# Later loads of x^T and u, and one-hot blocks of 32 columns in bursts of four sets, in a gated mix of a Fourier layer and a product-key expert layer

## The chip, the cores and the metric

The kernel runs on one core of one Trainium2 chip. The metric is the device time of one execution in microseconds (us). A core has TensorE (PE in the profile; its weight loads are shown apart as PEld), VectorE (DVE), ScalarE (ACT), GpSimd (POOL) and SyncE (SP), which here only issues transfers. All work from instruction streams of their own, in order, and wait for one another by semaphores.

## The reference

For x of 2048 tokens by 640 the output is g A + (1 - g) B, a gate for each token between two layers:

```python
g = _sigmoid((x * gate_w).sum(-1, keepdims=True))
# A: Fourier mixing
a = jnp.einsum("bsd,ed->bse", x, dft_hid_re)
b = jnp.einsum("bsd,ed->bse", x, dft_hid_im)
y = jnp.einsum("ts,bse->bte", dft_seq_re, a) - jnp.einsum("ts,bse->bte", dft_seq_im, b)
# B: 32 heads, two key tables of 16, 256 experts
q = jnp.einsum("nd,dhc->nhc", xf, w_q)
s1 = jnp.einsum("nhd,ed->nhe", q1, k1)
s2 = jnp.einsum("nhd,ed->nhe", q2, k2)
...  # the two best of 16 in each table, the two best of the 4 sums, their expert numbers top_e
g = _softmax(top_s, axis=-1)
act = _gelu(jnp.einsum("nd,nhkd->nhk", xf, u[top_e]))
out = jnp.einsum("nhk,nhk,nhkd->nd", g, act, v[top_e])
```

## The kernel before

All large products are made of fp32 values split into two fp32r parts, high and low, with three matmuls each (`mm3`, L141): 128 weight columns by 512 moving columns. TensorE's stream is written out by hand and is nearly one unbroken row of them.

**The main loop.** `pieces` are 128 steps (two DFT matrices, four column blocks of 512 tokens, 16 row blocks). `seq_piece(n)` issues the load of piece n + 5, the split of piece n + 3 (ScalarE copies the high part, GpSimd, or a GpSimd transfer that adds, makes the low one) and 15 matmuls. After each piece, `follow(n)` runs whatever `at(n, f)` has entered for that piece, in the order of entry. The instruction order of every engine and queue follows from this.

**Work between the pieces, first stage (pieces 0 to 29).** The weights W of the scores (w_q times the keys) are made in eight groups of four loads: `load_wq` brings 640 KB each on SP's queue into one of five buffers, `w_part` makes 8 small matmuls (L380; 32 weight columns by 320 moving columns) from each, `split_w` and `make_t` split the result. Group G stands at piece 6 + 3G, the last at 27. Beside them stand the row blocks of x being stored for later (`put_x`), the load of x^T's first pair of token blocks (`load_xT(0)`, at piece 21), its split (`split_xT`, 27) and sums (`sum_xT`, 28), and the five blocks of u's table (`load_u(k)` at pieces 21 to 25 into two small buffers, `split_u(k)` two pieces later).

**Second stage (to about piece 66).** `score_step` makes the scores of two token blocks in four steps, `topk` picks on VectorE, `gates` and `weigh` turn the picks into three rows for each choice: a bit for the first index, a bit for the second, a weight. `rows(b)` transposes them by transfers into `ROWS[0]` and `ROWS[1]` (tokens 0 to 1023 and 1024 to 2047), the last of them spaced out by `bg.space`.

**Third stage: `experts()`.** The sums of weights for each token and expert are made by matmuls of one-hot blocks. A chunk is 64 tokens of a half (`todo`: 2 halves of 16 chunks). `build` makes a set for one chunk with three VectorE operations over 1024 fp16 elements (L845): compare the first bits with a table of 16 powers, compare the second bits, multiply the first by the weights. The innermost dimension holds 4 tokens beside one another. `use` runs a group of sets as one burst of matmuls (L857), 16 for each set, 64 weight columns by 64 moving columns (16 indices by 4 tokens on both sides), with outputs at partitions 0 or 64. Only the blocks in which a token meets itself count: `mask` (L815) multiplies by a mask on ScalarE, four operations for each chunk, and `add_up` (L821) reduces over the 4 tokens on VectorE into `cd`. There are four sets (`free_sets`, `HOT`); a group has three of them, and the next set is built before the group's burst is issued. `store_gates` stores `cd` to DRAM with two transfers for each half. Near the end (`ending`, piece 121 on) sets 2 and 3 are given up and groups have two sets.

**The pump.** Third-stage work is not placed by piece. `run_bg(0.68)` after every three matmuls adds 0.95 x 0.68 us to a credit; a generator such as `experts()` issues its next step whenever the credit is above 0, and each `yield` says what the step costs (0.8 us, later 1.05, for an operation of `build`; 0.75 for an `add_up`). `experts()` starts with a debt of 3.0. Other VectorE work lowers the credit too (`bg.credit -= ...`). So the place of a burst in TensorE's stream is fixed when the program is made, by these prices, and not by when VectorE is done.

**Fourth stage.** After piece 127 two times 42 steps with the hidden DFT and v's table make the output.

Of the kernel before, what the change touches and what calls it, by code (L numbers as in the profile page):

```python
# [33 lines left out]
NB = 4  # L34
GSCALE = 32768.0
# [4 lines left out]
NSTEP = 7 * KZ  # L40
AHEAD = 5
AWAY = 11
BYPASS = 4
ACCUM_END = NT * (NC + 2) - 4

# [61 lines left out]
def gated_mix_kernel(ctx: ExitStack, tc: tile.TileContext, xT, xn, dreT, dimT, wsre, wsim, wq, kT, uT, vv, gw, out):  # L107
    nc = tc.nc
    ctx.enter_context(tc.manual_schedule())

    const = ctx.enter_context(tc.tile_pool(name="const", bufs=1))
    big = ctx.enter_context(tc.tile_pool(name="big", bufs=1))
# [37 lines left out]
    gd = [dram.tile([2, 4, E, E, P], F32, name=f"gd{g}", tag=f"gd{g}") for g in range(2)]  # L150
# [4 lines left out]
    def run_bg(us):  # L155
# [6 lines left out]
    UH, UL = (WU[:, 2 * NW + n * KD * NE:2 * NW + (n + 1) * KD * NE].rearrange("p (k c) -> p k c", k=KD)  # L162
              for n in range(2))
# [32 lines left out]
    def at(n, f, *args):  # L196
        then.setdefault(n, []).append(lambda: f(*args))
# [4 lines left out]


    banks = []
    p3, last_part, ending, closing, early, share = None, False, False, False, True, 0.95
    grow, staged, P22 = {}, {}, {}

    def load_row(q):
# [40 lines left out]
    for q in range(2 * NC):  # L249
        n = NT * (q + 1)  # L250
# [10 lines left out]
    p1 = p1_stack.enter_context(tc.tile_pool(name="p1", bufs=1, reuse_waits="tile"))  # L261
# [77 lines left out]
    wtab4 = const.tile([P, E, 4], F16)  # L339
    powers = const.tile([P, E], F16)  # L340
    top_bits = const.tile([P, 1], F32)
    mask4 = const.tile([P, 4], F32)

    def put_keys():
        for r in range(2):
# [6 lines left out]
    def make_tables():  # L352
        for e in range(E):
            nc.gpsimd.memset(powers[:, e:e + 1], 2.0 ** (E - 1 - e))
        nc.gpsimd.memset(top_bits, INF)
        nc.gpsimd.tensor_copy(wtab4, powers[:, :, None].to_broadcast([P, E, 4]))
        nc.vector.tensor_reduce(mask4, identf.rearrange("p (a b) -> p b a", b=4), op=OP.add, axis=AX.X)
        nc.vector.tensor_scalar(mask4, mask4, 1.0 / GSCALE, None, op0=OP.mult)

    for n, f in ((2, put_keys), (4, make_ident), (9, make_tables)):  # L360
        at(n, f)
# [3 lines left out]
    WQB = 5  # L365
# [48 lines left out]
        for n in range(1, 5):  # L414
            split(t[:, n - 1], *(w[:, :, c] for w in TW[n]), nc.vector)

    uf = {}

    def load_u(k):
        uf[k] = p1.tile([P, NE], F32, name="uf", tag="uf", bufs=2)  # L420
        nc.sync.dma_start(uf[k], uT[k])

    def split_u(k):
        split(uf.pop(k), UH[:, k], UL[:, k], nc.vector)


    xf, xs = {}, {}
# [58 lines left out]
    for G in range(NG):  # L486
        b = 6 + 3 * G
# [19 lines left out]
    def gate():  # L507
# [18 lines left out]
    ROWS = [cp.tile([P, 3, P, 8], F16, name=f"rows{g}") for g in range(2)]  # L526
# [251 lines left out]
    for n in range(2 * NT + 3, 4 * NT + 3):  # L778
        s = n % NT
# [12 lines left out]

    def store_gates(g):
        if g in summed and g not in stored:
            for s in range(2):
                nc.sync.dma_start(gd[g][s].rearrange("t e f m -> e t f m"), summed[g][64 * s:64 * s + 64])
            stored.add(g)

    free_sets = deque(range(4))
# [2 lines left out]
    def experts():  # L802


        shp = [P, 16, E, 4]
        wt = wtab4[:, None].to_broadcast(shp)
        todo = deque((g, c) for g in range(2) for c in range(16))
        cd = {}

        masked, unmasked = deque(), deque()  # L810

        def mask(t):
            f = t.rearrange("p m (e t) -> p (m e) t", t=4)
            for n in range(4):
                nc.scalar.activation(f[:, :, n], f[:, :, n], AF.Copy, scale=mask4[:, n:n + 1])  # L815

        def add_up(g, c, t):
            if c == 0:
                store_gates(g - 1)
                cd[g] = p3.tile([P, E, P], F32, name="cd", tag="cd")  # L820
            nc.vector.tensor_reduce(cd[g][:, :, 8 * c:8 * c + 8].rearrange("p e m -> p m e"),  # L821
                                    t.rearrange("p m (e t) -> p m e t", e=E), op=OP.add, axis=AX.X)
            if c == 15:
                summed[g] = cd[g]

        def settle(force=False):
            us = 0.0
            if masked:
                add_up(*masked.popleft())
                us = 0.75  # L830
            if unmasked and (force or not closing):
                masked.append(unmasked.popleft())
                mask(masked[-1][2])
            return us

        def build(g, c, s):
            pt, qt = (HOT[s // 2][:, s % 2, n].rearrange("p (m e t) -> p m e t", e=E, t=4) for n in range(2))

            def row(n):
                r = ROWS[g][:, n, 8 * c:8 * c + 8, :].rearrange("p b (s t) -> p (b s) t", t=4)  # L840
                return r[:, :, None, :].to_broadcast(shp)

            assert rowed >= set(range(8 * g, 8 * g + 8))
            for o, a, b, op in ((pt, row(0), wt, OP.is_equal), (qt, row(1), wt, OP.is_equal), (pt, pt, row(2), OP.mult)):
                nc.vector.tensor_tensor(o, a, b, op=op)  # L845
                yield (0.8 if early else 1.05) + settle()

        def use(group):
            assert not last_part
            while masked or unmasked:  # L850
                yield settle(True)
            for i, (g, c, s) in enumerate(group):
                t = bank((6, 7, 5)[i], (P, 8, E * 4))
                pt, qt = (HOT[s // 2][:, s % 2, n].rearrange("p (m c) -> p m c", m=16) for n in range(2))
                for m in range(16):
                    r = slice(64 * (m % 2), 64 * (m % 2) + 64)
                    nc.tensor.matmul(t[r, m // 2, :], pt[:, m], qt[:, m], start=True, stop=True)  # L857
# [372 lines left out]
    prep_split = {NPC - 4: (0,), NPC - 3: (1,), NPC - 2: (2,), NPC - 1: (3, 4)}  # L1230
    WP = None
    for n in range(N0, NPC):
        ending, closing, early = n >= NPC - 7, n % NT == NT - 1, n < ACCUM_END
        seq_piece(n)
        follow(n)
        if n >= N1 and p3 is None and NT // NB - 1 in gated:
            p2_stack.close()
            p3 = ctx.enter_context(tc.tile_pool(name="p3", bufs=1, reuse_waits="tile"))
            pools.append(p3)
            HOT.append(p3.tile([P, 2, 2, 16 * E * 4], F16, name="hot0"))  # L1240
            HOT.append(p3.tile([P, 2, 2, 16 * E * 4], F16, name="hot1", tag="WP"))
            bg.add(experts(), late=True)
            bg.credit -= 3.0
        if n == NPC - 4:
            bg.drain(lambda: {2, 3} <= set(free_sets))
            HOT.pop()
# [57 lines left out]
```

## Time and profile before

| | us |
|---|---|
| median of 3 runs (749.87 to 751.22) | 750.1 |
| the profiled execution | 750.43 |
| its span on the core | 748.7 |
| W products, TensorE (L380, 256 matmuls) | 19.1 busy |
| one-hot matmuls (L857, 512) | 10.2 busy |
| one-hot builds, VectorE (L845, 64 and 32 operations) | 57.8 and 31.6 busy |
| masks, ScalarE (L815, 128) | 43.1 busy |
| reductions, VectorE (L821, 32) | 21.7 busy |

The span is what the profiler sees on the core; the execution's time has a little around it. A matmul's shown length is longer than its distance to the next one, since matmuls are pipelined; distances between starts are what the stream costs. In the row of a group, `x512 | 10.2, 197 | 0.0` means 512 instructions, 10.2 us busy in total, 197 ns mean of one, and no idle time of the engine ahead of them. "SPq" is SyncE's queue of transfers.

### The profile page before, as it was taken

The numbers are of one execution on the slowest core, as the hardware profiler recorded it, in microseconds if no ns is written. First come the engines' busy times: TensorE is split into PE (matmuls) and PEld (weight loads), VectorE is DVE, ScalarE is ACT, GpSimd is POOL, SyncE is SP. The second block draws the span as 40 slices with busy tenths as digits, with TensorE's granted clock in tenths as the row PEclk, the third lists the DMA queues.
The fourth block names the chain that finished last, engine by engine and source line by source line (L and its number), as shares of the span: only waits on it lengthen the run. The fifth ranks groups of instructions, "written<-read, shape, count | busy, mean of one in ns | idle before, by whom it ended". The sixth has DMA issues, their size and how long they took to land.

```text
span 748.7 us, 11141 instructions
## 1 busy us (share of the span) xinstructions
PE 743.8 (99%) x3925; PEld 603.8 (81%) x3925; DVE 585.7 (78%) x741; ACT 365.9 (49%) x664; POOL 342.4 (46%) x286
## 2 busy tenths in 40 slices
PE   9999999999999999999999999999999999999998
PEld 7777767888888888888888888888888888888887
DVE  6964098495999899999999888979899974357651
ACT  4325234543544745555463686633545653443451
POOL 5533325440532424145235456643455793487253
PEclk9999999999999999999999999999999999999999
DMA  9999999777556786972398766488876689775301
GB/s 333 392 380 364 344 374 354 231 222 250 129 176 141 190 242 157 237 200 79 114 395 285 162 168 188 133 255 280 266 234 197 222 262 343 219 239 172 113 29 71
DMA packets 84488, 171.11 MB, mean 229 GB/s; under 512 B 16080, under 2 KB 21328, under 8 KB 84176
## 3 DMA queue, kind: packets, MB, share of 16 engines
q1 hardware_dynamic: 70960, 146.13, 57.9%
q0 software_dynamic: 5472, 9.96, 8.5%
q10 hardware_dynamic: 8000, 14.31, 5.2%
q8 instruction: 31, 0.51, 0.3%
q14 instruction: 25, 0.20, 0.1%
HBM read 136.40 MB, written 32.39 MB: 225 GB/s over the span
## 4 chain that ended last, share of the span: by engine, by line
PE 94%; DMA 5%; SPq 0%; DVE 0%; ACT 0%; issue 0%; ACTq 0%
PE b L143 30%; PE b L145 30%; PE b L144 30%; PE b L239 2%; DMA wf<-in_wsre 2%; PE b L380 2%; DMA wq<-in_wq 1%; PE b L857 1%; DMA xd<-X 1%; DMA gdr<-gc 1%; DVE wp L386 0%; SPq L177 0%; ACT WS L295 0%; ACTq L514 0%; DVE ST L1191 0%
## 5 line engine op out<-in xcount | busy, mean ns | idle before, releaser
L143 PE MATMUL b<-WS,X 128*128 128x512 f32 x620 | 243.3, 392 | 0.0
L144 PE MATMUL b<-WS,X 128*128 128x512 f32 x620 | 241.4, 389 | 0.0
L145 PE MATMUL b<-WS,X 128*128 128x512 f32 x620 | 241.3, 389 | 0.0
L139 POOL TENSOR_TENSOR WS<-wf,WS 128x512 fp32r<-128x512 f32 x89 | 131.9, 1486 | 168.3 <-ACT WS L138 151.8
L143 PEld LDWEIGHTS b<-WS,X 128*128 128x128 f32 x620 | 116.3, 188 | 28.2 <-issue 4.1
L145 PEld LDWEIGHTS b<-WS,X 128*128 128x128 f32 x620 | 116.4, 188 | 24.4
L144 PEld LDWEIGHTS b<-WS,X 128*128 128x128 f32 x620 | 116.4, 188 | 23.6
L138 ACT ACTIVATE WS<-wf 128x512 fp32r<-128x512 f32 x89 | 55.5, 626 | 69.0 <-PE b L145 40.9
L845 DVE TENSOR_TENSOR hot<-rows,wtab 128x1024 f16<-128x1024 f16 x64 | 57.8, 930 | 4.3 <-PE b L857 4.3
L139 POOL TENSOR_TENSOR xl<-xf,xh 128x640 fp32r<-128x640 f32 x16 | 27.2, 1702 | 72.0 <-ACT xh L138 72.0
L567 ACT ACTIVATE sc<-b 128x512 f32<-128x512 f32 x32 | 19.9, 621 | 80.8 <-PE b L145 77.0
L191 POOL DMA_DIRECT2D WS<-in_wsre x30 | 26.4, 881 | 61.8 <-ACT WS L189 60.5
L139 POOL TENSOR_TENSOR WS<-ra,WS 128x512 fp32r<-128x512 f32 x33 | 47.1, 1439 | 14.3 <-ACT WS L138 14.1
L815 ACT ACTIVATE b<-b,mask 128x128 f32<-128x128 f32 x128 | 43.1, 342 | 14.9 <-PE b L857 11.8
L138 ACT ACTIVATE WS<-ra 128x512 fp32r<-128x512 f32 x47 | 29.4, 631 | 42.4 <-PE b L145 29.6
L622 DVE TENSOR_TENSOR eq<-sc,mm 128x1024 f16<-128x1024 f32 x32 | 44.4, 1387 | 0.9
L629 DVE TENSOR_REDUCE tied<-eq 128x64 f32<-128x1024 f16 x32 | 39.0, 1219 | 0.9
L620 DVE TENSOR_REDUCE mm<-sc 128x64 f32<-128x1024 f32 x32 | 38.7, 1211 | 0.2
L139 POOL TENSOR_TENSOR WP<-ra,WP 128x512 fp32r<-128x512 f32 x13 | 19.2, 1490 | 31.0 <-ACT WP L138 30.9
L217 DVE SCALAR_TENSOR_TENSOR ST<-ST,grow 128x512 f32<-128x512 f32 x40 | 31.7, 855 | 1.7 <-ACT tw L138 1.7
L845 DVE TENSOR_TENSOR hot<-hot,rows 128x1024 f16<-128x1024 f16 x32 | 31.6, 986 | 0.0
L143 PE MATMUL b<-WU,xh 128*128 128x512 f32 x80 | 31.1, 389 | 0.0
(209 smaller groups left out, 1449.1 us busy)
## 6 DMA issues: line engine op xcount, KB each, us to landing
X<-xd SPq DMA_DIRECT2D x36, 640.0 KB, 6.5
wq<-in_wq SPq DMA_DIRECT2D x32, 640.0 KB, 7.1
wf<-in_wsim SPq DMA_DIRECT2D x64, 256.0 KB, 4.8
wf<-in_wsre SPq DMA_DIRECT2D x63, 256.0 KB, 6.4
ra<-pd SPq DMA_DIRECT2D x40, 256.0 KB, 3.3
pd<-ST ACTq DMA_DIRECT2D x35, 256.0 KB, 5.6
WS<-in_wsre POOLq DMA_DIRECT2D x30, 256.0 KB, 6.0
xd<-X SPq DMA_DIRECT2D x11, 640.0 KB, 9.1
```

The lines of the kernel that those rows point to most:

```text
L138: nc.scalar.activation(h, f, AF.Copy)
L139: eng.tensor_sub(l, f, h.bitcast(F32))
L143: nc.tensor.matmul(o, wh, ah, start=first, stop=False, skip_group_check=more)
L144: nc.tensor.matmul(o, wh, al, start=False, stop=False, skip_group_check=more)
L145: nc.tensor.matmul(o, wl, ah, start=False, stop=last, skip_group_check=more)
L191: nc.gpsimd.dma_start(l, (wsre, wsim)[w][c, s], accum_op=OP.add)
L217: nc.vector.scalar_tensor_tensor(f, f, -1.0 if w else 1.0, g, op0=OP.mult, op1=OP.mult)
L620: nc.vector.tensor_reduce(m, sc, op=OP.max, axis=AX.X)
L622: nc.vector.tensor_tensor(eq, sc, m[:, :, None].to_broadcast([P, HH, E]), op=OP.is_equal)
L629: nc.vector.tensor_reduce(tied[:, s, ib, :], eq, op=OP.add, axis=AX.X)
L815: nc.scalar.activation(f[:, :, n], f[:, :, n], AF.Copy, scale=mask4[:, n:n + 1])
L845: nc.vector.tensor_tensor(o, a, b, op=op)
```

## The change

There are two independent edits.

The first moves x^T's first pair and u's table. The pair's load goes from piece 21 to 25, where it stands behind the last of W's loads in SP's queue, its split from 27 to 28, its sums from 28 to 29. u's five loads of 128 KB become one of 640 KB at piece 25 into one of W's five buffers, and its five splits become one at piece 27.

The second changes the one-hot blocks. With `TB = 2` the innermost dimension holds 2 tokens instead of 4, so that a set's matmuls are 32 of 32 weight columns by 32 moving columns, at output partitions 0, 32, 64 and 96 (`CG = 4`). Two sets fill one bank. A group has four sets, with two in the ending, and the banks rotate. The mask has two operations for two chunks, the reduction one for two chunks, the store four transfers for each half. A fifth set may be added (`free_now`): for the first half of the tokens in the space of `xl`, if all rows are placed and the piece is before 86 (`late`), for the second half over `ROWS[0]`, as soon as no set of the first half is left to build. The price of an operation of `build` goes from 0.8 to 0.9 in the early part, and `settle` is called once for each set instead of three times.

```diff
+TB = 2
+MS = 64 // TB
+CG = P // (TB * E)
...
-    uf = {}
-
-    def load_u(k):
-        uf[k] = p1.tile([P, NE], F32, name="uf", tag="uf", bufs=2)
-        nc.sync.dma_start(uf[k], uT[k])
-
-    def split_u(k):
-        split(uf.pop(k), UH[:, k], UL[:, k], nc.vector)
+    uf = []
+
+    def load_u():
+        f = p1.tile([P, 4, HALF], F32, name="wq", bufs=WQB).rearrange("p a b -> p (a b)").rearrange("p (k c) -> p k c", k=KD)
+        nc.sync.dma_start(f, uT.rearrange("k p c -> p k c"))
+        uf.append(f)
+
+    def split_u():
+        split(uf.pop(), UH, UL, nc.vector)
...
-    at(n - 8, load_xT, 0)
-    for k in range(KD):
-        at(n - 8 + k, load_u, k)
-        at(n - 6 + k, split_u, k)
+    at(n - 4, load_xT, 0)
+    at(n - 4, load_u)
+    at(n - 2, split_u)
     for a in range(2):
-        at(n - 2, split_xT, 0, a)
-    at(n - 1, sum_xT, 0)
+        at(n - 1, split_xT, 0, a)
+    at(n, sum_xT, 0)
...
-            for n in range(4):
-                nc.scalar.activation(f[:, :, n], f[:, :, n], AF.Copy, scale=mask4[:, n:n + 1])
+            for n in range(TB):
+                nc.scalar.activation(f[:, :, n], f[:, :, n], AF.Copy, scale=mask_t[:, n:n + 1])
...
+        def free_now():
+
+            if todo[0][0] == 1:
+                if not HOT[4:] or HOT[4][0] == 0:
+                    if HOT[4:] and 4 not in free_sets:
+                        return [s for s in free_sets if s < 2 or not ending]
+                    if not HOT[4:]:
+                        HOT.append(None)
+                        free_sets.append(4)
+                    HOT[4] = 1, ROWS[0].rearrange("p a b c -> p (a b c)")[:, :16 * P].rearrange("p (n c) -> p n c", n=2)
+            elif not HOT[4:] and not late and len(rowed) == NT:
+                HOT.append((0, big.tile([P, 2, 16 * P // 2], F16, name="hot4", tag="xl")))
+                free_sets.append(4)
+            return [s for s in free_sets if s not in ((2, 3) if ending else (4,) if late and todo[0][0] == 0 else ())]
...
-                yield (0.8 if early else 1.05) + settle()
+                yield (0.9 if early else 1.05) + (settle() if op == OP.mult else 0.0)
...
-                t = bank((6, 7, 5)[i], (P, 8, E * 4))
-                pt, qt = (HOT[s // 2][:, s % 2, n].rearrange("p (m c) -> p m c", m=16) for n in range(2))
-                for m in range(16):
-                    r = slice(64 * (m % 2), 64 * (m % 2) + 64)
-                    nc.tensor.matmul(t[r, m // 2, :], pt[:, m], qt[:, m], start=True, stop=True)
-                unmasked.append((g, c, t))
+                if i % 2 == 0:
+                    t = bank(5 + rotate("hot", 3), (P, 16, E * TB))
+                    unmasked.append((g, c, t))
+                pt, qt = (f.rearrange("p (m c) -> p m c", m=MS) for f in pair(s))
+                for m in range(MS):
+                    r = slice(TB * E * (m % CG), TB * E * (m % CG + 1))
+                    nc.tensor.matmul(t[r, 8 * (i % 2) + m // CG, :], pt[:, m], qt[:, m], start=True, stop=True)
...
-            while todo and len(group) < (2 if ending else 3):
-                free = [s for s in free_sets if s < 2 or not ending]
-                if prev and (not free or ending and any(s > 1 for g, c, s in prev)):
+            while todo and (len(group) < (2 if ending else 4) or len(group) % 2):
+                free = free_now()
+                if prev and (not free or ending and any(s in (2, 3) for g, c, s in prev)):
...
+        ending, closing, early, late = n >= NPC - 7, n % NT == NT - 1, n < ACCUM_END, n >= NT * (NC + 2) - 10
```

More of the change, by code (lines that the diff above doesn't have):

```diff
@@ L204, in gated_mix_kernel @@
     banks = []
-    p3, last_part, ending, closing, early, share = None, False, False, False, True, 0.95
+    p3, last_part, ending, closing, early, late, share = None, False, False, False, True, False, 0.95
     grow, staged, P22 = {}, {}, {}
@@ L355, in make_tables @@
         nc.gpsimd.memset(top_bits, INF)
[L356 to L358 removed]
+        nc.gpsimd.tensor_copy(wtab, powers[:, :, None].to_broadcast([P, E, TB]))
+        nc.vector.tensor_reduce(mask_t, identf.rearrange("p (a b) -> p b a", b=TB), op=OP.add, axis=AX.X)
+        nc.vector.tensor_scalar(mask_t, mask_t, 1.0 / GSCALE, None, op0=OP.mult)
     for n, f in ((2, put_keys), (4, make_ident), (9, make_tables)):
@@ L794, in store_gates @@
         if g in summed and g not in stored:
-            for s in range(2):
-                nc.sync.dma_start(gd[g][s].rearrange("t e f m -> e t f m"), summed[g][64 * s:64 * s + 64])
+            for s in range(CG):
+                n, t = divmod(TB * s, 4)
+                nc.sync.dma_start(gd[g][n, t:t + TB].rearrange("t e f m -> e t f m"),
+                                  summed[g][TB * E * s:TB * E * (s + 1)])
             stored.add(g)
@@ L802, in experts @@
     def experts():
-        shp = [P, 16, E, 4]
-        wt = wtab4[:, None].to_broadcast(shp)
+        shp = [P, MS, E, TB]
+        wt = wtab[:, None].to_broadcast(shp)
         todo = deque((g, c) for g in range(2) for c in range(16))
@@ L1232, in gated_mix_kernel @@
     for n in range(N0, NPC):
-        ending, closing, early = n >= NPC - 7, n % NT == NT - 1, n < ACCUM_END
+        ending, closing, early, late = n >= NPC - 7, n % NT == NT - 1, n < ACCUM_END, n >= NT * (NC + 2) - 10
+        assert n < NT * (NC + 2) - 1 or not HOT[4:] or HOT[4][0] or 4 in free_sets
         seq_piece(n)
@@ L1239, in gated_mix_kernel @@
             pools.append(p3)
-            HOT.append(p3.tile([P, 2, 2, 16 * E * 4], F16, name="hot0"))
-            HOT.append(p3.tile([P, 2, 2, 16 * E * 4], F16, name="hot1", tag="WP"))
+            for t in ("hot0", "WP"):
+                f = p3.tile([P, 2, 2, 16 * E * 4], F16, name="hot", tag=t)
+                HOT.extend(f[:, a] for a in range(2))
             bg.add(experts(), late=True)
```

19 lines of the change are left out of this document (11 added, 8 removed).

## The prediction

> **What bounds the kernel now.** I read the page's first part, the chain that ended last, the windows of 12 us, and then the starts of TensorE's instructions where they become irregular.
>
> ```profile
> span 748.7 us, 11141 instructions
> PE 743.8 (99%) x3925; PEld 603.8 (81%) x3925; DVE 585.7 (78%) x741; ACT 365.9 (49%) x664; POOL 342.4 (46%) x286
> PE 94%; DMA 5%; SPq 0%; DVE 0%; ACT 0%; issue 0%; ACTq 0%
> 84.00:96.00 12.00, 12.00 (x76) 8.71 (x75) 1.34 (x3) 2.45 (x5) 3.86 (x3) 1.00 1.02 414
> 96.00:108.00 12.00, 11.31 (x72) 7.90 (x70) 11.86 (x21) 3.67 (x9) 4.21 (x3) 1.00 0.98 374
> ```
>
> A window row gives its bounds and length, the busy time of PE, PEld, DVE, ACT and POOL, the granted clock, the DMA share and GB/s. TensorE is busy for 743.8 of 748.7 us, and of these two windows the second lacks 0.69 us of it. So an edit pays only where it takes time out of TensorE's own stream or a wait out of TensorE; work saved on the others is worth nothing by itself. Two places of that stream are touched:
>
> ```profile
> 97.25 10.08 DMA wq<-in_wq
> 104.86 1.82 PE L380 MATMUL b<-wq,kp 128*32 128x320 f32 x24
> 107.37 0.74 PE L380 MATMUL b<-wq,kp 128*32 128x320 f32 x8 [0.69 <-DMA wq<-in_wq]
> 108.05 0.50 PE L143 MATMUL b<-WS,X 128*128 128x512 f32 x1
> 118.55 2.29 PE b L380 x32
> ...
> 419.32 0.39 PE L145 MATMUL b<-WS,X 128*128 128x512 f32 x1
> 419.64 0.95 PE L857 MATMUL b<-hot 128*64 128x64 f16 x48
> 420.52 0.50 PE L143 MATMUL b<-WS,X 128*128 128x512 f32 x1
> 420.85 0.39 PE L144 MATMUL b<-WS,X 128*128 128x512 f32 x1
> ...
> 586.79 0.39 PE L145 MATMUL b<-WS,X 128*128 128x512 f32 x1
> 587.10 0.69 PE L857 MATMUL b<-hot 128*64 128x64 f16 x32
> 587.73 0.50 PE L143 MATMUL b<-WS,X 128*128 128x512 f32 x1
> 588.07 0.39 PE L144 MATMUL b<-WS,X 128*128 128x512 f32 x1
> 588.30 0.40 PE L145 MATMUL b<-WS,X 128*128 128x512 f32 x1
> ```
>
> A row's first number is a start, its second a length; lengths overlap, so I use starts. First place: group 6 of the W products has 32 matmuls, the last 8 of which wait for W's load 27. It takes 108.05 - 104.86 = 3.19 us, the next group 2.29: **0.90 us are lost**. Second place: the one-hot bursts. Ordinary matmuls start 0.23 us apart (588.07 to 588.30). The burst of 48 takes 420.85 - 419.32 - 2 x 0.23 = 1.07 us out of the stream, the burst of 32 takes 588.07 - 586.79 - 0.46 = 0.82. Sixteen matmuls therefore cost 0.25 us, 16 ns each, and each burst has a fixed 1.07 - 0.77 = 0.30 us. There are 512 matmuls in ten bursts of 48 and one of 32: 8.2 + 3.3 = **11.5 us**.
>
> **Part 1, loads behind W's last weights.**
>
> ```profile
> 92.96 0.87 SPq L371 DMA_DIRECT2D wq<-in_wq  x2
> 93.92 0.85 SPq L433 DMA_DIRECT2D xf<-in_xT  x2
> 94.82 0.42 SPq L421 DMA_DIRECT2D uf<-in_uT  x1
> 97.25 2.00 SPq L371 DMA_DIRECT2D wq<-in_wq  x2
> 106.63 0.33 SPq L421 DMA_DIRECT2D uf<-in_uT  x1
> 107.59 0.86 SPq L371 DMA_DIRECT2D wq<-in_wq  x2
> 113.53 0.42 SPq L371 DMA_DIRECT2D wq<-in_wq  x1
> SPq L421 <- DVE tt L408: 4.0, 2, 3.3
> ```
>
> Counted back from load 31 at 113.53, the two issues from 97.25 are loads 27 and 28, and 27 lands at 107.33 by the chain. Two xT issues (128 x 640 fp32, 0.33 MB each) and u's first (0.13 MB) stand ahead of it: 0.79 MB, 2.1 us at the 374 GB/s of that window. Without them it lands near 105.2. Its matmuls would begin at 104.86 + 0.75 x 2.29 = 106.6, so the whole 0.90 us goes and 1.4 us of slack stays. What is late next is load 31, for the last group. It too comes forward, because SP no longer stands in line at u's buffer (4.0 us in the last row): its own buffer was last read by group 6's third quarter. I take **-0.9**; if another transfer keeps load 27 late it is 0, and more than 0.9 isn't there to gain.
>
> Moved past: the two xT issues, five u issues that become one of 0.66 MB, five ACT copies and five VectorE subtractions that become one each, and xT's split and sums one piece later. u's new buffer was last read by load 27's matmuls, so SP waits for nothing beyond about 107; behind it stand pieces' loads, which have two pieces (6.8 us) in hand. ScalarE's split of u waits for a transfer that now starts with the last W loads, and behind it stand xT's split and W_seq pieces' copies, three pieces ahead of their matmuls. The price is nothing while those leads last; if u or xT lands 3 us too late it is up to 1.5 us, for the scores that start four pieces later.
>
> **Part 2, blocks of 32 columns.**
>
> ```profile
> L380 PE MATMUL b<-wq,kp 128*32 128x320 f32 x256 | 19.1, 436 | 0.7 <-DMA wq<-in_wq 0.7
> ```
>
> There are twice as many matmuls (1024) with 32 weight columns and 32 moving columns each, now four beside one another instead of two: 256 rounds before and after. A round costs 2 x 16 = 32 ns now. At the stream's rate (0.23 us for 512 columns, 0.45 ns each) 64 columns are 29 ns of it, and 3 ns are fixed. No row shows a round of 32 fp16 columns. Bounds: half a round, 16 ns (4.1 us saved); or 16 ns for each matmul as now, 64 ns a round (8.2 us lost). The nearest row for four beside one another is the W product above: 32 matmuls of 320 fp32 columns in 2.29 us, eight rounds of four, 72 ns for each, although one lasts 436. The number of instructions isn't the price there; columns are. I take columns plus the fixed part, 14.5 + 3 = 17.5, say 18 ns: 256 x 14 = **-3.6**.
>
> The Trainium skill, "TensorE: Matmul & The Clock Gate", section "Wait — 56ns, not 53.3ns?", says that starts never come closer than about 25 ns however few the columns. The 48 matmuls here, 16 ns apart on average, show that this can't hold across matmuls in different columns of the array; whether it holds for a round no run here shows. Read as a floor for a round, it would save 256 x 7 = 1.8 us instead of 3.6 (an estimate from that page).
>
> **Part 3, bursts of four sets.** 32 chunks in fours make 8 bursts, not 11: 3 x 0.30 = **-0.9** (9 bursts, if the last ones break up near the end: -0.6). The evacuation shrinks: 32 masking operations instead of 128 on ScalarE, 16 reductions instead of 32 on VectorE, both off the path, and that helps a little in Part 4.
>
> **Part 4, what a burst waits for.** Before, three sets are used after a fourth has been built, so VectorE may lag one set. The fifth set would keep that up, but it can't for the first half: it is allowed before piece 86 and only when all rows are placed.
>
> ```profile
> 422.71 2.53 ACT L246 ACTIVATE ST<-b 128x512 f32<-128x512 f32 x5
> 453.14 1.93 ACT L721 ACTIVATE rows<-lb 128x384 f16<-128x384 f16 x1
> 417.62 1.78 DVE L845 TENSOR_TENSOR hot<-hot,rows 128x1024 f16<-128x1024 f16 x1
> 420.52 0.68 DVE L845 TENSOR_TENSOR hot<-hot,rows 128x1024 f16<-128x1024 f16 x1
> 445.72 0.88 PE b L857 x48
> 446.58 0.68 DVE L845 TENSOR_TENSOR hot<-hot,rows 128x1024 f16<-128x1024 f16 x1
> L845 DVE TENSOR_TENSOR hot<-rows,wtab 128x1024 f16<-128x1024 f16 x64 | 57.8, 930 | 4.3 <-PE b L857 4.3
> L845 DVE TENSOR_TENSOR hot<-hot,rows 128x1024 f16<-128x1024 f16 x32 | 31.6, 986 | 0.0
> L845 DVE TENSOR_TENSOR hot<-rows,wtab x64: 674/681/2248, 410.1 to 572.3; 128x1024 f16<-128x1024 f16 x64
> L627 DVE TENSOR_TENSOR eq<-eq,powers x32: 678/692/3415, 155.5 to 396.7; 128x1024 f16<-128x1024 f16 x32
> L622 DVE TENSOR_TENSOR eq<-sc,mm x32: 1210/1225/2544, 151.7 to 395.5; 128x1024 f16<-128x1024 f32 x32
> ```
>
> The five copies at 422.71 close piece 79, which ends near 424. A piece is 15 x 0.23 = 3.4 us, so piece 86 starts near 424 + 6 x 3.4 + 2 bursts = 446.6; the last row is placed at 453.14. So chunks 0 to 15 run on four sets, all four go into each burst, and bursts 1 to 3 have nothing built ahead; from the fourth on, set five (over the first half's rows) restores the lag.
>
> Burst 1: the twelfth operation (420.52 + 0.68) ends at 421.2. The pump pays 0.9 instead of 0.8 for each of 12 operations, and spends 0.65 in each 0.68 us of products: with the 3.0 that it starts in debt, 13.8 of credit instead of 12.6 put the burst two steps later, at 419.32 + 0.23 + 1.36 = 420.9. With the signal's way it waits some 0.5 us. Bursts 2 and 3: before, the operation that the after kernel would wait for ended 1.5 us behind burst 3 (446.58 + 0.68 against 445.72), and 12 x 0.1 = 1.2 us of added price covers most of it; I take 0.5 each. That is **+1.5**; from 0 to a whole set for each burst (three operations of 0.93 us, the mean of the 96: 57.8 + 31.6 us): 8.4.
>
> The price of an operation itself: runs of two equal-stepped fp16 elements instead of four. Runs of four (L845, 681 ns) and of sixteen (L627, 692 ns) cost the same, so I take the same for two; the other bound is L622's 1225 ns.
>
> **Sum**, against the profiled execution (750.43 us, of which 748.7 are span): -0.9 - 3.6 - 0.9 + 1.5 = -3.9, so 746.5. The median of the runs is 750.1, 0.3 below, and the forecast goes with it: **746.3**. Its own range, from the smaller terms: 744.5 to 748.0.
>
> **Rivals.**
> 1. A round has a floor. Whatever fills a round beside its columns may not shrink with them; the 3 ns fixed speak against, and that no round under 64 columns is in the trace speaks for. Midway between 18 and 32 ns, 25 ns: 746.3 + 256 x 0.007 = 748.1. The Trainium skill's rule above would bring it about.
> 2. Bursts 1 to 3 wait for VectorE (slower than before). For: no lookahead, lags up to 1.5 us, and single operations of 1.78 us among the builds (417.62). Against: the higher price and fewer reductions. At a whole set for each burst +8.4 instead of +1.5: 753.2. It decides the sign from 1.8 us a burst on (3 x 1.8 covers -5.4).
> 3. Each matmul keeps its 16 ns, because the stream is bound by instructions: 746.3 + 3.6 + 8.2 = 758.1. Against: the W products.
> 4. Runs of two fall to L622's rate: 96 x 0.54 = 52 us more on VectorE. A group of 12 grows by 6.5 us against a spacing of 13 us, so the four early bursts would wait some 4 us each: about 762.
> 5. It doesn't do what it says: load 27 stays late and the fourth burst finds no fifth set either: +0.9 and +0.5, 747.7, inside the forecast's range.
>
> **How the numbers follow.** Forecast with rival 5: 0.53; rival 1: 0.22; rival 2: 0.14; rival 3: 0.06; rival 4: 0.05. About 0.2%, 1.5 us, is what can be told from no change: faster means below 748.6, slower above 751.6. Faster: 0.53 and 0.10 of rival 1's; same: the rest of rival 1, and 0.07 of rival 2; slower: the rest. So 0.63, 0.19, 0.18. The range leaves out rivals 3 and 4 and the ends of others: half rounds without any wait, 746.3 - 0.5 - 1.5 = 744.3, and rival 2 short of its end, 752.5.
>
> **What would show it.** No wait for wq near 105, and groups 6 and 7 both at 2.29 us. Eight bursts, each 0.30 us plus 128 x 4.5 ns = 0.9 us; rival 3 would show 2.4. The weight loads of bursts 1 to 3 idle for under 1 us each on the builds' last operation, those of later bursts not at all. Operations of the builds at 0.68 us when alone. I'm wrong if TensorE gets a new wait near 122 to 140 us (u, xT, scores), if builds run at 1.2 us, or if the pieces behind a burst wait for ScalarE's copies.

## The result and the profile after

The change makes the kernel slower: 753.89 us against 750.11 (medians of 8 runs each), ratio 1.0052 [1.0039, 1.0065]. The forecast was 746.3 us, with a range whose ends the prediction works out as 744.3 and 752.5, so the result lies above it, and the change goes the other way. The profiled execution took 753.65 us; the one before 750.43. Three executions of 1252 to 1738 us in the later comparisons count in the medians, which they move by 0.1 us at most, but not in the ratios.

The page of the changed kernel, first part and the shares of the chain that ended last:

```profile
span 751.9 us, 12032 instructions
PE 745.9 (99%) x4437; PEld 606.4 (81%) x4437; DVE 579.0 (77%) x721; ACT 337.0 (45%) x564; POOL 344.0 (46%) x286
PE 96%; DMA 2%; SPq 1%; ACT 0%; POOL 0%; issue 0%; DVE 0%; ACTq 0%
```

ScalarE has 28.9 us less to do and VectorE 6.7, as planned, and neither is worth anything. TensorE's busy time went up by 2.1 us. The two places that the forecast was about, in TensorE's timeline (start, length, then the number of instructions; the last three rows are answers for windows that end at 439.78, 439.98 and 440.18, so their counts are the matmuls begun until then):

```profile
105.76 2.36 PE L383 MATMUL b<-wq,kp 128*32 128x320 f32 x32
108.05 0.50 PE L146 MATMUL b<-WS,X 128*128 128x512 f32 x1
...
439.27 0.39 PE L148 MATMUL b<-WS,X 128*128 128x512 f32 x1
439.58 1.26 PE L883 MATMUL b<-hot 128*32 128x32 f16 x128
440.78 0.50 PE L146 MATMUL b<-WS,X 128*128 128x512 f32 x1
441.11 0.39 PE L147 MATMUL b<-WS,X 128*128 128x512 f32 x1
...
439.58 0.37 PE L883 MATMUL b<-hot 128*32 128x32 f16 x30
439.58 0.57 PE L883 MATMUL b<-hot 128*32 128x32 f16 x53
439.58 0.77 PE L883 MATMUL b<-hot 128*32 128x32 f16 x74
```

Group 6 of the W products is whole: 108.05 - 105.76 = 2.29 us, so its wait of 0.90 us is gone. The burst of 128 takes 441.11 - 439.27 - 0.46 = 1.38 us where 0.9 were forecast. The counts say why: 30 matmuls begin in the first 0.2 us, then 23 and 21 in the next two. By the single starts, 32 matmuls go in rounds of four, 25 ns a round, and all behind them one by one, 8.3 ns apart, with a gap of 31 ns ahead of the last matmul of the second, third and fourth set. All eight bursts take 11.53 us; the eleven of before took 11.64. Of the 4.5 us that Parts 2 and 3 were to save, 0.1 is there, and 0.4 if the slow clock that the third burst meets is taken out.

What costs is a new stop at piece 88. Its rows in the timeline, and the windows around it (bounds, busy time of each engine, granted clock, DMA share, GB/s):

```profile
453.17 0.39 PE L146 MATMUL b<-WS,X 128*128 128x512 f32 x1
455.42 0.50 PE L147 MATMUL b<-WS,X 128*128 128x512 f32 x1 [1.87 <-DMA WS<-in_wsim]
```

```profile
456.00:458.00 2.00, 2.00 (x131) 1.78 (x131) 1.43 (x1) 1.33 (x3) 1.99 (x2) 0.74 0.70 163
458.00:460.00 2.00, 2.00 (x6) 1.52 (x5) 2.00 (x3) 0.00 (x0) 1.23 (x1) 0.50 0.95 239
460.00:462.00 2.00, 2.00 (x9) 1.64 (x8) 2.00 (x4) 0.24 (x1) 0.00 (x0) 0.91 0.53 143
```

TensorE stands still for 455.42 - 453.17 - 0.23 = 2.0 us, and then runs at a lower clock: 2 us each at 0.74, 0.50 and 0.91 are 1.7 us lost. In this pair of profiles the sum closes: start-up +0.9 (the 61st ordinary matmul starts at 19.19 us instead of 18.29, more on it below), group 6 -0.9, bursts without the slow clock in them -0.4, stop +2.0, clock +1.7: +3.3, against 751.9 - 748.7 = 3.2. The clock's share differs from run to run: the mean granted clock of the eight runs lies between 0.995 (the two of 756.6 and 756.8 us) and 1.000 (two, of 752.8 and 753.2 us).

The chain that ended last shows where the stop comes from:

```profile
440.35 6.48 DMA wf<-in_wsim
...
446.90 0.33 ACTq L230
...
449.62 5.76 DMA WS<-in_wsim
...
455.42 0.50 PE b L147
```

Read backwards: the accumulating transfer that makes piece 88's low part (L194, on GpSimd's queue) goes out at 449.62, behind DD's subtraction on GpSimd (448.10), DD's copy on ScalarE (447.28) and the two copies of piece 88 (447.92); ScalarE stands at a store ahead of these (L230, block 4's fourth, to pd) until 446.9; and that store is released by the load of piece 89, with which it shares no data. The trace's records name the semaphores: the store waits for number 100, on which it is to count itself, and the load issued at 440.35 counts its completion on number 100. All transfers of SyncE and ScalarE share eight such semaphores, handed out in turn in an order that is fixed when the kernel is built. In before, the same store had the semaphore of a row transpose issued at 434.79, and went out at 441.4.

### The profile page after: what moved, and what is told of

Same layout as the page of the kernel before. It is cut to its first block, busy times and chain, and to the rows that moved or that the text cites. A ratio compares the mean times of both kernels' runs of the same rounds, so it can differ in the third digit from the quotient of the medians.

```text
span 751.9 us, 12032 instructions
## 1 busy us (share of the span) xinstructions
PE 745.9 (99%) x4437; PEld 606.4 (81%) x4437; DVE 579.0 (77%) x721; ACT 337.0 (45%) x564; POOL 344.0 (46%) x286
## 4 chain that ended last, share of the span: by engine, by line
PE 96%; DMA 2%; SPq 1%; ACT 0%; POOL 0%; issue 0%; DVE 0%; ACTq 0%
PE b L146 30%; PE b L147 30%; PE b L148 30%; PE b L383 2%; PE b L242 2%; PE b L883 1%; DMA wf<-in_wsim 1%; DMA WS<-in_wsim 1%; PE b L329 1%; SPq L719 0%; ACT rows L724 0%; POOL DD L142 0%; SPq L921 0%; SPq L180 0%; ACT DD L141 0%
## 5 line engine op out<-in xcount | busy, mean ns | idle before, releaser
L869 DVE TENSOR_TENSOR hot<-rows,wtab 128x1024 f16<-128x1024 f16 x56 | 54.1, 1000 | 12.4 <-PE b L883 12.4
L194 POOL DMA_DIRECT2D WS<-in_wsre x30 | 26.3, 878 | 61.0 <-ACT WS L192 59.7
L220 DVE SCALAR_TENSOR_TENSOR ST<-ST,grow 128x512 f32<-128x512 f32 x40 | 33.9, 902 | 0.6 <-ACT ST L249 0.6
L147 PE MATMUL b<-WU,xh 128*128 128x512 f32 x80 | 31.1, 389 | 0.0
L146 PE MATMUL b<-WU,xh 128*128 128x512 f32 x80 | 31.1, 389 | 0.0
L148 PE MATMUL b<-WU,xl 128*128 128x512 f32 x80 | 31.1, 389 | 0.0
```

The lines of the kernel that those rows point to most:

```text
L146: nc.tensor.matmul(o, wh, ah, start=first, stop=False, skip_group_check=more)
L147: nc.tensor.matmul(o, wh, al, start=False, stop=False, skip_group_check=more)
L148: nc.tensor.matmul(o, wl, ah, start=False, stop=last, skip_group_check=more)
L194: nc.gpsimd.dma_start(l, (wsre, wsim)[w][c, s], accum_op=OP.add)
L220: nc.vector.scalar_tensor_tensor(f, f, -1.0 if w else 1.0, g, op0=OP.mult, op1=OP.mult)
```

## The experiments

The median of before over all these comparisons was 750.1 to 750.4 us.

**Which part loses (e1_loads_only, e2_blocks_only).** e1 has only the part with the loads, e2 only the blocks and bursts. The core of e1 against before:

```diff
-    at(n - 8, load_xT, 0)
-    for k in range(KD):
-        at(n - 8 + k, load_u, k)
-        at(n - 6 + k, split_u, k)
+    at(n - 4, load_xT, 0)
+    at(n - 4, load_u)
+    at(n - 2, split_u)
     for a in range(2):
-        at(n - 2, split_xT, 0, a)
-    at(n - 1, sum_xT, 0)
+        at(n - 1, split_xT, 0, a)
+    at(n, sum_xT, 0)
```

> The kernel before with the first edit alone (x^T's first pair and u's table loaded behind W's last weights). Theory 1 (the lost time is one stall of TensorE near piece 88, made by the second edit: a store on ScalarE's queue stands behind an unrelated weight load): no stall, group 6 of the W products back to 2.29 us, 749.2 us (748.6 to 750.2). Theory 2 (the stall comes from the first edit, because four transfers fewer shift which transfers share a completion semaphore): the stall is here, 752.5 to 753.5 us.

> The second edit alone (blocks of 32 columns, bursts of four sets, fifth set), with the loads of the kernel before. Theory 1: the stall near 453 us is here, 2 us of waiting and 1.5 us of half clock behind it, and the 0.9 us of group 6 come back: 753.5 to 754.8 us. Theory 2: no stall, 750.0 us.

e1: 751.29 us, ratio 1.0011 [1.0003, 1.002], 1.1 us above its forecast's range. e2: 753.01 us, 1.0042 [1.0028, 1.0056], 0.5 below its range. So the stop belongs to the blocks: e2 has it in full (2.0 us, `WS<-in_wsim`), e1 not at all. But e1 doesn't win either. In its chain:

```profile
111.06 11.77 DMA wq<-in_uT
...
122.86 0.69 ACT WU L138
...
137.33 0.88 DVE xf L456
...
138.95 0.49 ACT b L567
...
139.49 0.50 PE b L143
```

u's table takes 11.8 us to land; ScalarE's split of it, then VectorE's subtraction of 1.5 us, hold up the sums of W's parts; x^T's split stands behind those on ScalarE (129.5 instead of 122.6), its four sums on VectorE begin at 133.5 instead of 130.4, the splits of these sums follow, and ScalarE's copy between two score products comes behind them. TensorE waits 0.7 us by the view of waits, and 0.88 by the starts of its matmuls, which is nearly all that had been saved. Of the eight profiles with this order of splits, the changed kernel's alone has no such wait; in the other seven it is 0.2 to 1.4 us by the starts.

**x^T ahead of u (e6_loads_order).**

```diff
-    at(n - 2, split_u)
     for a in range(2):
-        at(n - 1, split_xT, 0, a)
-    at(n, sum_xT, 0)
+        at(n - 2, split_xT, 0, a)
+    at(n - 1, sum_xT, 0)
+    at(n, split_u)
```

> The first part of the change alone, with x^T's split and sums one piece earlier, ahead of u's split (x^T split at n - 2, its sums at n - 1, u split at n). Order theory (the wait of about 1 us near 139 us comes because x^T's split stood behind u's on ScalarE and behind the sums that u's split had held up on VectorE): that wait goes, the wait in W's group 6 stays away, 749.5 us (749.2 to 749.9), against 751.3 for the part as it was and 750.4 before. Landing theory (the loads behind W's last weights take 10 to 12 us to land, and that is what is late in any order): the wait stays at 0.5 us or more, 750.3 to 751.3.

The wait is gone: the only wait of TensorE in this view (line, what it waited for, us in total, times, longest) is the one at the start.

```profile
PE b L326 <- PEq L1296: 0.8, 1, 0.8
```

The order theory holds for the wait, and e9 and e10 below, with the same order, don't have it either. The time is 750.39 us, ratio 0.9995 [0.9986, 1.0003]: 0.9 us better than e1, but level with before, and above the forecast of 749.2 to 749.9. Its profiled execution, at 749.64, was the fastest of its runs, and there the stream stands 1.0 us ahead of before's from group 6 to the last burst.

**Is before's wait always there (e11_before_again)?**

> The kernel before, unchanged, for a second profile: is the wait of 0.90 us in the sixth group of W's products there in every execution, and how much does the clock's phase at the start move from one execution to the next? If the wait is there, the gain of 0.9 us that the mended first part shows in its trace is real, and 750.39 against 750.39 is a scatter of starts or a cost elsewhere; if it is absent, before itself has runs without it, and the gain was never 0.9 us on the median.

It is, and it varies:

```profile
PE b L380 <- DMA wq<-in_wq: 1.4, 1, 1.4
```

This execution took 751.14 us. So the wait in group 6 is real in both profiles of before (0.69 and 1.4 us by this view); e2, with the old loads, shows 1.0. That its removal leaves no trace in the medians stays unexplained. The scatter of before's runs (749.5 to 751.9) is more than twice the effect, and e6's interval, which reaches 1.0 us below before, doesn't exclude it.

**What a burst costs (e4_wide_moving, e5_bursts_of_two).** e4 gives 28 of each set's 32 matmuls 64 moving columns; what the second half computes is overwritten by a later matmul of the set. e5 uses bursts of two sets.

```diff
-                    nc.tensor.matmul(t[r, 8 * (i % 2) + m // CG, :], pt[:, m], qt[:, m], start=True, stop=True)
+                    j = 8 * (i % 2) + m // CG
+                    w = E * TB if m // CG == 7 else 2 * E * TB
+                    o = t.rearrange("p a c -> p (a c)")[r, E * TB * j:E * TB * j + w]
+                    nc.tensor.matmul(o, pt[:, m], pair(s)[1][:, E * TB * m:E * TB * m + w], start=True, stop=True)
```

```diff
-            while todo and (len(group) < (2 if ending else 4) or len(group) % 2):
+            while todo and (len(group) < 2 or len(group) % 2):
```

> The changed kernel with 64 instead of 32 moving columns in 28 of every 32 one-hot matmuls; the second half of each goes to where the next matmul writes and is overwritten. If columns at 0.45 ns are the price of a round, as the prediction had it, a burst grows from 1.39 us by 28 rounds of 14 ns, to 1.8, and the bursts together by 3.1 us. If the supply of instructions is the price (8.3 ns for a weight load and its matmul, seen behind the first 34 matmuls of a burst), a burst stays within 0.1 us of 1.39.

> The changed kernel with bursts of two sets (16 bursts of 64 matmuls of 32 columns) in place of four. A burst of 128 took 1.39 us, of which 1.09 us between its first and last start: the first 34 starts in rounds of four of 25 ns, the others 8.3 ns apart. Supply theory (matmuls queued ahead go out at 25 ns a round, and behind them the engine starts them only as fast as it is handed new ones, 8.3 ns each): 0.21 + 30 x 0.0083 + 0.30 = 0.76 us for a burst of 64, 12.2 us for all. Floor theory (25 ns a round throughout, the rest is lost where one set follows another): 16 x 0.025 + 0.30 = 0.70 us, 11.2 us for all. Flat theory (33 ns a round throughout): 0.83 us, 13.3 us for all. The stall at piece 88 may go or stay, as the bursts come at other pieces: no forecast of the time.

e4 (751.78 us, one run), a burst in TensorE's timeline:

```profile
439.07 0.39 PE L148 MATMUL b<-WS,X 128*128 128x512 f32 x1
439.39 1.28 PE L886 MATMUL b<-hot 128*32 128x64 f16 x128
440.60 0.50 PE L146 MATMUL b<-WS,X 128*128 128x512 f32 x1
440.93 0.39 PE L147 MATMUL b<-WS,X 128*128 128x512 f32 x1
```

440.93 - 439.07 - 0.46 = 1.40 us, against 1.38 with half the columns. By the single starts the early rounds take 29 ns instead of 25, and the later ones 33 as before. So the moving columns cost next to nothing in these bursts. Their price goes with the number of matmuls, or with the weight loads, which e4 leaves at 32 columns each; no run parts these two. e5 (754.05 us, one run):

```profile
439.78 0.39 PE L148 MATMUL b<-WS,X 128*128 128x512 f32 x1
440.10 0.68 PE L883 MATMUL b<-hot 128*32 128x32 f16 x64
440.71 0.51 PE L146 MATMUL b<-WS,X 128*128 128x512 f32 x1
441.05 0.40 PE L147 MATMUL b<-WS,X 128*128 128x512 f32 x1
```

0.81 us for 64, 13.0 us for all sixteen. That lies between the supply theory (0.76) and the flat one (0.83) and well above the floor theory (0.70); the single starts decide: again 32 matmuls in 0.20 us and the other 32 in 0.30, the gap of 32 ns ahead of the last one included. Flat is wrong, and a floor of 25 ns throughout is wrong. A fixed rate of weight columns is wrong too, since the first eight rounds load as many as the others.

**How the stop comes about (e3_stores_on_sp, e7_dd_on_vector, e8_rows_later, e12_one_more_transfer).** Four links of the chain, one undone in each. e3 takes block 4's stores off ScalarE's queue:

```diff
-        eng = nc.sync if q == 2 * NC - 1 else nc.scalar
+        eng = nc.sync if q in (NC, 2 * NC - 1) else nc.scalar
```

> The changed kernel with the five stores of block 4 (pieces 81 to 85) issued on SP's queue instead of ScalarE's. Theory 1: ScalarE no longer stands still from 442 to 447 us, TensorE doesn't stall at piece 88, 749.2 to 750.3 us. Theory 3 (W's split is late because VectorE's unbroken builds shut GpSimd out, with one subtraction of 5.5 us instead of 1.6): that subtraction is still there and so is the stall, 753 to 754 us.

750.51 us, ratio 1.0004 [0.9995, 1.0014]: 3.4 us back, 0.2 above the range of theory 1. Eight of its runs lie at 749.5 to 750.8 and three at 752.3 to 752.8. The profiled one is of the three: TensorE still waits 1.5 us for the same transfer, because ScalarE's copy of piece 88 (L191) waits 4.8 us for the piece's load, which lands at 447.9. So the held store is one way in which a delay comes through, and the load of piece 88 is another.

What delays that load? One candidate is GpSimd: DD's subtraction, in the changed kernel and then in before (start, length; in brackets the idle time ahead and its releaser):

```profile
426.05 5.55 POOL L142 TENSOR_TENSOR DD<-draw,DD 128x640 fp32r<-128x640 f32 x1 [3.68 <-ACT DD L141]
```

```profile
425.95 1.56 POOL L139 TENSOR_TENSOR DD<-draw,DD 128x640 fp32r<-128x640 f32 x1 [1.84 <-ACT DD L138]
```

It takes 5.55 us while VectorE runs without a pause from 425.88 to 430.69; in before, VectorE waited 2.35 us for ScalarE's masks just there. The other candidate is SyncE's queue, the changed kernel first and then before:

```profile
439.34 1.50 SPq L180 DMA_DIRECT2D wf<-in_wsim  x2
441.31 4.06 SPq L719 DMA_TRANSPOSE lb<-lb  x3
```

```profile
438.46 0.86 SPq L177 DMA_DIRECT2D wf<-in_wsim  x2
443.71 3.65 SPq L716 DMA_TRANSPOSE lb<-lb  x3
```

With half the masks ScalarE places a slice's rows at 439.35 instead of 441.75, and the next row transposes, which need the place that this frees, go out 0.5 us behind the loads of pieces 88 and 89 (the expectations call them 87 and 88) instead of 4.4. The first of the two lands 6.6 us after its issue, at 445.9; in before 5.3 us after it, at 443.8. e7 and e8 part the two candidates:

```diff
-        split(draw[m][:, a], DD[:, w, 0, k], DD[:, w, 1, k], nc.gpsimd)
+        split(draw[m][:, a], DD[:, w, 0, k], DD[:, w, 1, k], nc.vector if (m, a) == (1, 1) else nc.gpsimd)
```

```diff
-            bg.space(lambda a=a: step(a), 5.0 if a else 16.0 if b == NT // NB - 1 else 8.0)
+            bg.space(lambda a=a: step(a), (5.0 if b < NT // NB - 1 else 7.0) if a else 16.0 if b == NT // NB - 1 else 8.0)
```

> The changed kernel with one subtraction (the second half of DD's step m = 1, which took 5.55 us on GpSimd) moved to VectorE. Lock-out theory (that GpSimd operation, shut out while VectorE runs seven operations without a pause, holds up the loads and additions behind it until TensorE stops at piece 88): the stop of 2.0 us and the slow clock behind it go, 750.2 to 750.8. Transposes theory (ScalarE has half the masking to do, copies a slice's rows 2.4 us earlier, so the row transposes go out right behind the loads of pieces 87 and 88 and slow them): the stop stays, 753 to 754.

> The changed kernel with the steps of the last four slices' row transposes and copies 7.0 us apart in place of 5.0 (nothing else). Transposes theory (the transposes go out 0.5 us behind the loads of pieces 87 and 88, and these land at 446.8 us in place of 443.8): with the transposes elsewhere, the loads land in time, ScalarE is not held at the store, the stop at piece 88 goes, 750.2 to 750.8. Lock-out theory: the GpSimd operation of 5.55 us is still there and the stop stays, 753 to 754.

e7: 752.38 us, 1.0028 [1.0016, 1.004], between both forecasts. e8: 751.10 us, 1.0008 [0.9999, 1.0017], 0.3 above the range of the transposes theory. ScalarE in e7, then GpSimd and ScalarE in e8:

```profile
447.06 0.74 ACT L141 ACTIVATE DD<-draw 128x640 fp32r<-128x640 f32 x1 [5.31 <-DMA wf<-in_wsim]
```

```profile
426.01 5.41 POOL L142 TENSOR_TENSOR DD<-draw,DD 128x640 fp32r<-128x640 f32 x1 [3.67 <-ACT DD L141]
...
441.23 0.33 ACTq L230 DMA_DIRECT2D pd<-ST  x1
```

Without the long operation on GpSimd, ScalarE still stands for 5.3 us and TensorE still stops, for 1.2 us, with the clock at 1.00. With the transposes elsewhere the long operation is still there, and there is no stop. So GpSimd's long operation is real, but the chain doesn't need it; that VectorE's work makes it long is read from the timelines alone. e8 moved two things, though: the load of piece 88 now goes out at 433.1, ahead of a set of transposes, and the store's semaphore is another one, long free. e12 leaves the order of the transfers and moves that store to the next semaphore, by one transfer of 4 bytes in between (which moves all transfers behind it on by one, too):

```diff
+    spare = dram.tile([1, 1], F32, name="spare")
...
             nc.sync.dma_start(pf[n], (wsre, wsim)[w][c, s])
+            if n == 89:
+                nc.sync.dma_start(spare, zc[:1, :1])
```

> The changed kernel with one more transfer, of 4 bytes, on SyncE's queue between the load of piece 89 and the next row transposes (its value is used nowhere). Transfers count their completion on eight semaphores, handed out in turn; the store that holds ScalarE until 446.9 us has the semaphore of a load issued at 440.35, and one transfer more in between gives it the next one, that of the store of 438.37. Semaphore theory (the stop at piece 88 comes from this sharing alone): the store goes out by 442.5, the transposes still follow the loads by about 0.5 to 1.5 us, the loads still land at 446 to 447, and the stop and the slow clock go: 750.2 to 750.9 us. Transposes theory (the loads, slowed by the transposes, stop TensorE in one way or another): the stop stays at 1 us or more, 752 to 754.

751.32 us, 1.0017 [1.0007, 1.0028], between both forecasts, with the widest scatter of all (749.96 to 754.5). ScalarE in its profile:

```profile
442.87 0.33 ACTq L233 DMA_DIRECT2D pd<-ST  x1
...
446.01 0.63 ACT L194 ACTIVATE WS<-wf 128x512 fp32r<-128x512 f32 x1 [2.02 <-DMA wf<-in_wsim]
```

The store is free, and 2.6 of the 3.8 us are back. What is left is the load of piece 88: it takes 6.9 us to land, ScalarE waits 2.0 us for it, and the accumulating transfer behind it, issued at 447.71 instead of 449.62, lands 1.1 us too late. So the stop has two causes: the shared semaphore with the larger share, and piece 88's load. That load takes 3.8 to 5.4 us in the four profiles with the old blocks (before twice, e1, e6). With transposes at most 1.3 us behind the pair of loads it takes 6.2 to 7.5 us in seven profiles, and 5.4 in e5. That the transposes slow it fits most of this, but no run moved them alone. In the five other profiles in which ScalarE issues that store and TensorE stops there for 1 us or more, the store shares its semaphore with a piece's load; in none of the rest does it.

**Both parts mended (e9_both_mended, e10_rows_later_order).** e9 is the change with e3's and e6's edits, e10 with e8's and e6's.

> The changed kernel with both mends: block 4's stores on SyncE's queue, and x^T's split and sums one piece earlier, ahead of u's split. The stores alone brought it to 750.51 us. If the wait near 139 us costs in the changed kernel what it cost in the first part alone (751.29 against 750.39 without it), 749.6 us (749.2 to 750.1). If the mended order only moves a wait about, 750.5. In either case the stop at piece 88 should come in few runs.

> The changed kernel with the last slices' rows 7.0 us apart (751.1 us alone) and x^T's split and sums one piece earlier, ahead of u's split. No stop at piece 88, no wait near 139 us: 750.2 us (749.8 to 750.7). What is then left between it and before is the sum of the two parts when nothing waits: group 6 of W's products 0.9 us less, the bursts 0.1 to 0.4 us less by the starts of TensorE's matmuls, so 749.2 by the sum of the trace's terms; a median at or above 750.4 would say that a further cost is spread where no wait shows.

e9: 750.07 us, 0.9996 [0.9987, 1.0005], at the upper end of its first forecast. e10: 750.78 us, 1.0004 [0.9995, 1.0013], just above its range, with a wait of 0.4 us left there in its profile and bursts 1 and 2 at 1.58 and 1.71 us, in which a set isn't built in time. e9 shows no wait of TensorE beside the start, and bursts of 11.29 us in all. It is the best version of the change, and it can't be told from before.

One term of all these is explained in part. The 61st ordinary matmul starts at 18.58 to 19.31 us in the nine profiles of kernels with both parts, and at 18.19 to 18.54 in the five of the others. TensorE's first matmuls start 0.4 to 0.6 us apart as long as the granted clock hasn't gone up, and by the traces' clock records it goes up at 4.43 to 6.54 us in the nine and at 3.68 to 4.97 in the five. Counted from the first ordinary matmul, the 61st comes after 13.9 to 14.6 us in the nine and after 13.7 to 13.9 in the five. Why the clock goes up later isn't shown: nothing of the change lies there, and no run was made to find it.

## Why the prediction was wrong

**Part 1 (-0.9).** The mechanism was right: load 27 comes in time and the whole 0.90 us goes. The step that failed is the price of nothing for what is moved: "up to 1.5 us, for the scores that start four pieces later" was worked out and set aside, on the ground that the leads of the pieces would last. They did; what didn't is VectorE's and ScalarE's order behind u's split. e1 paid 0.88 of the 1.5 us, and e6 showed that the order of two splits decides it. In the changed kernel's own profile this wait is absent, so it is no part of the 3.2 us there.

**Part 2 (-3.6).** Wrong, the largest step. "Columns plus the fixed part, 18 ns" for a round: the first eight rounds of a burst take 25 ns, the others 33. e4 shows that the moving columns have next to no part in it (29 and 33 ns with twice as many). "The number of instructions isn't the price" was taken from the W products, where a matmul has 320 columns; from there it couldn't be known what happens at 32. Rival 3 named the resource that fits (the stream is bound by instructions, be they the matmuls or their weight loads) and the wrong price: a matmul costs 8.3 ns, not 16, so all of them take 8 x 1.09 = 8.7 us against the 8.2 that the prediction reckoned for before, and not 16.4. The Trainium skill, "TensorE: Matmul & The Clock Gate", section "Wait — 56ns, not 53.3ns?", says that starts never come closer than about 25 ns. Read as a floor for a round, that is what the first eight rounds of a burst show (25 ns), and the later ones are slower (33 ns). The Trainium skill, "TensorE: Matmul & The Clock Gate", section "Architectural detail: the array is 16× 32×32, not 1× 128×128", gives TensorE's queue a depth of 64. In the traces 32 matmuls with their 32 weight loads are 64 instructions, and behind the 32nd matmul the rate drops. That the queue is what runs dry fits both, but no run changed the number of loads.

**Part 3 (-0.9).** Its sum is right: each burst keeps a fixed 0.30 us (1.39 less the 1.09 between first and last start), and three fewer are there.

**Part 4 (+1.5).** Only burst 1 waits, and for 0.16 us (one gap of 157 ns); bursts 2 and 3 not at all. Rival 2, which was to carry the slower side, didn't come. The operation's price was right:

```profile
L869 DVE TENSOR_TENSOR hot<-rows,wtab x56: 674/683/2150, 410.2 to 546.4; 128x1024 f16<-128x1024 f16 x56
```

683 ns in the median, for runs of two as for runs of four.

**What was not seen.** The stop of 2.0 us and the 1.7 us of slow clock behind it, more than the whole of the loss. By the profiles the forecast is missed by three terms: this 3.7, the bursts with -0.4 in place of -3.0, and the 0.9 of the start-up, which the prediction didn't have. The step that failed here is in Part 3, which put the smaller evacuation down as off the path, at a price of nothing, and as a help. It is off the path, and it still changed the order of the transfers: the row transposes go out 2.4 us earlier, right behind two loads, and a store comes to share a semaphore with one of them, which passes a delay to ScalarE, GpSimd and TensorE in turn. The last sentence of the prediction listed copies that come late; these came early.

## What to carry to other kernels

Halving columns and doubling instructions gained only in the first 32 matmuls of a burst here: price a long burst of small matmuls by its count, from a row with matmuls as small. When an engine gets faster, ask what its earlier finish releases, and follow those transfers as if they had been added. And when a load is moved, look at the order on the engines that consume it, since a split put ahead of a more urgent one costs what the load saved.

## What the runs showed of the hardware

- Weight load and matmul of 32 columns: 32 of them in rounds of four every 25 ns, then one each 8.3 ns. With 64 moving columns the rounds take 29 ns, and the later pace is the same.
- The granted clock fell to 0.50 after a stop of 2.0 us (windows above). In e2 a stop of the same length left it at 1.00, and 1.2 us in e7 did too. The Trainium skill, "TensorE: Matmul & The Clock Gate", section "What's actually happening", puts an idle window of some 3.4 us ahead of a lower clock. The stop here was shorter, and its length alone doesn't decide.
- Where the stop falls fits what was seen. In all fourteen traces the recorded changes of the granted clock lie whole multiples of 3.41 us apart. In the changed kernel TensorE stands idle for 1.87 us of the stretch from 453.54 to 456.95, and the next stretch has half the clock. In e2 a border at 454.82 divides the stop, with 0.96 and 1.05 us idle on its sides. Over all traces, by TensorE's shown busy time, each of the 15 falls of the clock (14 of them at the very end) follows a stretch with 1.87 us or more of idle TensorE, and no stretch with 1.77 or less is followed by one.
- A GpSimd subtraction of 128x640 takes 1.56 us beside an idle VectorE and 5.55 us beside seven VectorE operations without a pause; VectorE's next three, beside GpSimd's next ones, took 1.5 to 2.2 us in place of 0.68.
- A store waits for a load that it shares no data with, when both count on one completion semaphore: ScalarE had no work for 5.2 us (442.04 to 447.28).
